# Five GpSimd transfers of weight rows, issued as single packets

## The chip, the cores and the metric

The kernel runs on one core of a Trainium2 chip. The metric is the device time of one execution in microseconds (us); less is better. The core has five engines with queues of their own: TensorE (PE) for matrix products, VectorE (DVE) and ScalarE (ACT) for elementwise work and reductions, GpSimd (POOL), and SyncE (SP), which here issues loads. Sixteen DMA engines move data between HBM and the on-chip memory. SyncE's transfers are queue q1 in the profile, GpSimd's are q0; both use the same sixteen engines.

## The reference

One decode step for 8 sequences with two branches on the same normalised input. Branch A is grouped-query attention over a cache of 4096 positions (32 query heads, 8 key/value heads of width 128); branch B is a gated MLP with 896 hidden units. All numbers are float32.

```python
xn = layernorm(x)                                   # x: 8 x 512
q  = xn @ wq                                        # 32 heads x 128
s  = softmax(q @ k_cache.T * 128**-0.5) @ v_cache   # per head; k, v: 8 x 8 x 4096 x 128
s  = s @ wo                                         # 8 x 512
z  = gelu(xn @ w_in)                                # 8 x 1792
z1, z2 = z[:896], layernorm(z[896:])
g  = silu((z1 * (w_sp * z2 + b_sp)) @ w_out)        # w_out: 896 x 512
out = x + s * g
```

The two caches are 268 MB of the 290 MB read.

## The kernel before

**Ring.** Large loads go through a ring of three slots of 64 KB per partition, 8.4 MB each over 128 partitions. SyncE issues the loads in program order: wq (slot 1), the MLP's weights (slot 2), kT(0,0) (slot 3), kT(0,1) (slot 1 again, once the query projection has read wq), v(0,0) (slot 2 again, once the MLP has read its weights), v(0,1), and so on for 8 heads, two halves each. `load_k` is lines 326 to 329, `load_v` lines 331 to 336. A load is issued when the last reader of the slot's earlier content is done.

**Order on TensorE.** `project_q(0)`, `project_q(1)` (lines 247 to 261), `mlp()` (167 to 245), then for each head `scores` (267 to 273), `softmax` and `values` (305 to 319). At the end the output projection with wo, whose last pieces are loaded in nine transfers of falling size.

**The MLP's slot** holds w_in, four of the seven 128-row blocks of w_out and a small side block. They come in one SyncE transfer, `w_mlp` (line 82). The other three blocks of w_out are taken out of it: the host packs their rows, as `w_ex`, into a region of the same slot (line 83), on partitions chosen row by row (the tables `LANES`, `ONES` and `RUNS`). Most of these rows come by four SyncE transfers (line 86). The rest come by five GpSimd transfers: `w_mid` (8 partitions of 14 KB, 112 KB) and `w_one0` to `w_one3` (3 partitions each, six pieces of 7 KB or 5 KB, so 42 or 30 KB). [...]

**Readers.** In `mlp()` the product with w_out is two loops: line 227 reads the four blocks of `w_mlp`, line 231 reads the seven units of `w_ex`. Line 231 is the last reader of the slot. Line 239 copies the side block on VectorE.

Of the kernel before, what the change touches and what calls it, by code (L numbers as in the profile page):

```python
# [14 lines left out]
B, D = 8, 512  # L15
# [9 lines left out]
QUAD = 4  # L25
# [20 lines left out]
def tile_gqa_gmlp_decode(ctx: ExitStack, tc: tile.TileContext, x, kT, v, wq, wo, w_mlp, w_ex0, w_ex1, w_ex2, w_ex3, w_mid, w_one0, w_one1, w_one2, w_one3, out, gate, stored):  # L46
    nc = tc.nc
# [27 lines left out]
    def from_slot(rows, n):  # L75
        lo = spare[0]
        spare[0] = lo + n
        return mlp_slot[:rows, lo:lo + n]
# [4 lines left out]
    w_ex = from_slot(P, UNITS * D).rearrange("p (u d) -> p u d", u=UNITS)  # L83
# [3 lines left out]
    turn = const.tile([4 * QUAD, 4, QUAD], F32, name="turn")  # L87
    queued = []

    def queue(dst, src):  # L90
        with tc.issue_after(queued[-1]) if queued else nullcontext():
            queued.append(nc.gpsimd.dma_start(dst, src).ins)

    def skip(i, k):
        queue(turn[:2 * k, i], w_mlp[:k, :4 * QUAD].rearrange("p (a q) -> p a q", a=2)[:, :, :QUAD])

    def one(i, src):
        p, u, n = ONES[i]
        queue(w_ex[p:p + 3, u:u + n].rearrange("p u d -> p (u d)").rearrange("p (c n) -> p c n", c=2),
              src[:, :3, :n * D // 2])  # L100

    skip(0, 7)
    queue(w_ex[60:68], w_mid[:, :QUAD])
    skip(1, 6)
    one(0, w_one0)
    skip(2, 7)
    one(1, w_one1)
    one(2, w_one2)
    skip(3, 6)
    one(3, w_one3)  # L110
# [242 lines left out]
    for h in range(HKV):  # L353
# [4 lines left out]
        for half in range(2):  # L358
# [11 lines left out]
            n = 2 if last else HALF  # L370
# [94 lines left out]
```

## Time and profile before

| | before |
|---|---|
| median of 3 runs | 689.87 us (689.77 to 689.96) |
| the profiled execution | 689.62 us, span 688.0 |
| granted TensorE clock, mean | 0.745 |
| PE busy | 341.1 us (50%) |
| read from HBM | 290.80 MB, 423 GB/s over the span |
| q1 (SyncE) | 6576 packets, 290.54 MB, 97.8% of 16 engines' span |
| q0 (GpSimd) | 656 packets, 0.27 MB, 0.1% |

The span runs from the first to the last instruction of the profiled execution; 1.6 us of its time lie around it. Times in the views count from the span's start. In the row of 40 slices each digit is the busy share of a slice of 17.2 us in tenths. In a group of instructions, the part behind the bar is busy time, mean ns of one, and the idle time just before, with what ended it. Line numbers are those of the kernel before.

### The profile page before, as it was taken

Reading aid. Unit: us, or ns where it says so; the run is one execution under the profiler, and the core shown is the slowest. Engines: PE = TensorE matmul, PEld = TensorE weight load, DVE = VectorE, ACT = ScalarE, POOL = GpSimd, SP = SyncE. Lnnn points to the kernel's source line nnn. Section 1 sums busy time; section 2 is a strip of 40 time slices with the busy share of each in tenths; the row PEclk is TensorE's granted clock in tenths of the full one; section 3 lists DMA queues with packets and bytes.
Section 4 is the critical chain, followed back from the end, with each engine's and each line's share of the span. In section 5 each row is a group of like instructions: output and inputs, shape, how many; then the busy total and the mean of one; then the engine's idle time right before and its main releaser. Section 6 shows DMA issues by size and latency. Waiting matters only on the chain.

```text
span 688.0 us, 5236 instructions
## 1 busy us (share of the span) xinstructions
PE 341.1 (50%) x2412; PEld 91.8 (13%) x2412; DVE 83.7 (12%) x163; ACT 13.4 (2%) x27; POOL 14.5 (2%) x26
## 2 busy tenths in 40 slices
PE   0353564555544445555544355555444445555558
PEld 0111121111111111111111011111101111111112
DVE  0133121100111021100201021100111021100221
ACT  0010000000000000000000000000000000000000
POOL 6100000000000000000000000000000000000000
PEclk9995597766776676777777667767776676777778
DMA  9999599999999999999999999999999999999997
GB/s 403 414 437 426 231 428 473 434 424 427 424 438 431 428 434 451 434 424 427 439 442 424 431 446 439 427 428 427 443 427 427 447 442 439 428 427 428 427 416 289
DMA packets 7397, 291.17 MB, mean 423 GB/s; under 512 B 1512, under 2 KB 1512, under 8 KB 2336
## 3 DMA queue, kind: packets, MB, share of 16 engines
q1 hardware_dynamic: 6576, 290.54, 97.8%
q8 instruction: 19, 0.31, 0.2%
q0 software_dynamic: 656, 0.27, 0.1%
q10 hardware_dynamic: 144, 0.03, 0.0%
q14 instruction: 2, 0.02, 0.0%
HBM read 290.80 MB, written 0.03 MB: 423 GB/s over the span
## 4 chain that ended last, share of the span: by engine, by line
DMA 73%; PE 18%; issue 4%; another core or an unknown queue 3%; DVE 1%; POOL 0%; SPq 0%; POOLq 0%
DMA slot<-in_kT 35%; DMA slot<-in_v 28%; PE sc L272 11%; DMA slot<-in_wo 7%; PE o_ps L313 6%; DMA slot<-in_x 3%; PE scr L227 1%; PE scr L231 1%; DVE slot L218 0%; PE scr L222 0%; POOL pick L134 0%; POOL slot L216 0%; SPq L335 0%; DVE rest L233 0%
## 5 line engine op out<-in xcount | busy, mean ns | idle before, releaser
L272 PE MATMUL sc<-slot,qz 128*32 128x512 f32 x1024 | 147.1, 739 | 127.0 <-DMA slot<-in_kT 127.0
L313 PE MATMUL o_ps<-slot,pT 128*16 128x512 f32 x1024 | 144.5, 728 | 110.5 <-DMA slot<-in_v 108.1
L272 PEld LDWEIGHTS sc<-slot,qz 128*32 128x32 f32 x1024 | 38.3, 132 | 229.3 <-issue 153.2
L313 PEld LDWEIGHTS o_ps<-slot,pT 128*16 128x16 f32 x1024 | 32.1, 112 | 208.8 <-issue 142.1
L277 DVE TENSOR_REDUCE nm<-sc 128x1 f32<-128x1024 f32 x8 | 9.8, 1225 | 271.2 <-PE sc L272 271.2
L316 DVE TENSOR_TENSOR o_all<-o_ps,diag 128x512 f32<-128x512 f32 x17 | 11.8, 692 | 241.7 <-PE o_ps L313 241.7
L279 ACT ACTIVATE p<-sc,nm 128x1024 f32<-128x1024 f32 x8 | 8.9, 1114 | 543.9 <-DVE nm L277 543.9
L323 PE MATMUL po_ps<-fold,o_sb 128*128 128x16 f32 x30 | 5.9, 273 | 26.8 <-DVE o_sb L318 26.8
L318 DVE TENSOR_REDUCE o_sb<-o_all 128x128 f32<-128x512 f32 x17 | 17.8, 1047 | 0.6
L162 PE MATMUL scr<-ident,slot 8*128 8x8 f32 x4 | 0.6, 255 | 28.0 <-DVE slot L159 28.0
L299 DVE STREAM_TRANSPOSE pT<-p 128x1024 f32<-128x1024 f32 x8 | 10.0, 1245 | 0.3
L323 PEld LDWEIGHTS po_ps<-fold,o_sb 128*128 128x128 f32 x30 | 4.5, 188 | 40.6 <-DVE o_sb L318 40.6
L252 PE MATMUL scr<-slot,xnT 128*32 128x512 f32 x64 | 9.7, 760 | 0.3 <-POOL slot L216 0.3
L231 PE MATMUL scr<-slot 128*32 128x512 f32 x14 | 3.6, 1058 | 11.8 <-DMA slot<-in_w_one 11.8
L347 PE MATMUL sc<-slot,oT 128*8 128x512 f32 (+1 forms) x60 | 8.2, 564 | 0.2 <-DMA slot<-in_wo 0.2
L282 PE MATMUL scr<-ident,nm 128*1 128x128 f32 x8 | 2.2, 270 | 10.8 <-DVE nm L277 10.8
L295 PE MATMUL scr<-wl,same 128*128 128x1 f32 x16 | 3.6, 297 | 6.5 <-DVE wl L293 6.5
L297 DVE TENSOR_SCALAR p<-p,w,wl 128x1024 f32<-128x1024 f32 x8 | 6.5, 813 | 0.3
L195 PE MATMUL scr<-part_sum,same 128*128 128x1 f32 x4 | 1.1, 348 | 8.4 <-DVE part_sum L193 8.4
L288 PE MATMUL scr<-ident,full 1*128 1x1 f32 x8 | 1.7, 219 | 5.1 <-DVE full L286 5.1
L162 PEld LDWEIGHTS scr<-ident,slot 8*128 8x128 f32 x4 | 0.5, 209 | 28.0 <-DVE slot L159 28.0
L295 PEld LDWEIGHTS scr<-wl,same 128*128 128x128 f32 x16 | 3.2, 249 | 7.0 <-PE scr L288 7.0
(97 smaller groups left out, 76.3 us busy)
## 6 DMA issues: line engine op xcount, KB each, us to landing
slot<-in_v SPq DMA_DIRECT2D x2, 4096.0 KB, 29.4
slot<-in_w_mlp SPq DMA_DIRECT2D x1, 4672.0 KB, 34.4
slot<-in_wo SPq DMA_DIRECT2D x1, 2048.0 KB
slot<-in_wo SPq DMA_DIRECT2D x1, 1536.0 KB
slot<-in_wo SPq DMA_DIRECT2D x1, 1280.0 KB, 39.7
slot<-in_wo SPq DMA_DIRECT2D x1, 1024.0 KB
slot<-in_wo SPq DMA_DIRECT2D x4, 256.0 KB, 19.1
slot<-in_wo SPq DMA_DIRECT2D x1, 768.0 KB
```

Source lines behind the costliest of these rows:

```text
L227: nc.tensor.matmul(pw[R * g:R * (g + 1), :], hT[:, R * g:R * (g + 1)], w_out_sb[:, g, :], start=True, stop=False)
L231: nc.tensor.matmul(pw[R * g:R * (g + 1), :], hE[:, i * R:(i + 1) * R], w_ex[:, i, :], start=False, stop=(i >= UNITS - G))
L252: nc.tensor.matmul(pq[R * g:R * (g + 1), :], xnT[:, k, :], wq_sb[:, k, lo:lo + REP * DH], start=(k == 0), stop=(k == NK - 1))
L272: nc.tensor.matmul(sc[R * g:R * (g + 1), c, :], qz[:, h, b * R:(b + 1) * R], k_sb[:, i, c, g, :], start=(b == 0), stop=(b == B - 1))
L277: nc.vector.tensor_reduce(m, sc, op=ALU.max, axis=AX.XY, negate=True)
L279: nc.scalar.activation(p, sc.rearrange("p c s -> p (c s)"), AF.Exp, bias=m, accum_out=l[:, h:h + 1])
L299: nc.vector.transpose(pT.rearrange("p j b g r -> p j g b r"), p.rearrange("p (j g b r) -> p j g b r", j=J, g=G, b=B))
L313: nc.tensor.matmul(of[R * c:R * c + G * REP, :], pT[:, j, b0 + i], v_sb[:, i, j], start=(j < rows), stop=(j >= J - rows))
L316: nc.vector.tensor_mul(o_all, o, diag[:, :, None].to_broadcast([P, G, DH]))
L318: nc.vector.tensor_reduce(o_sb, o_all.rearrange("p g d -> p d g"), op=ALU.add, axis=AX.X)
L323: nc.tensor.matmul(po[:, b0 * REP:(b0 + n) * REP], o_sb, f.rearrange("p i r -> p (i r)"), start=True, stop=True)
L347: nc.tensor.matmul(part[R * q:R * q + B, i * n:(i + 1) * n], oT[:, h, r, :], wo_sb[:, m, i * n:(i + 1) * n], start=(m < REP), stop=(cuts = ...
```

## The change

`queue` gets a third argument, `whole`, which it hands to the transfer as `single_packet`. It is set in the five transfers of w_out rows, `w_mid` and the four `w_one`, and not in the four `skip` transfers. [...] Sources, destinations, sizes and order stay, and on every engine the instructions stand in the same order as before.

```diff
-    def queue(dst, src):
+    def queue(dst, src, whole=False):
         with tc.issue_after(queued[-1]) if queued else nullcontext():
-            queued.append(nc.gpsimd.dma_start(dst, src).ins)
+            queued.append(nc.gpsimd.dma_start(dst, src, single_packet=whole).ins)
...
         queue(w_ex[p:p + 3, u:u + n].rearrange("p u d -> p (u d)").rearrange("p (c n) -> p c n", c=2),
-              src[:, :3, :n * D // 2])
+              src[:, :3, :n * D // 2], True)

     skip(0, 7)
-    queue(w_ex[60:68], w_mid[:, :QUAD])
+    queue(w_ex[60:68], w_mid[:, :QUAD], True)
     skip(1, 6)
     one(0, w_one0)
```

## The prediction

> **What bounds the kernel now.** I read the page first: its engine shares, the DMA row and the queues.
>
> ```profile
> PE 341.1 (50%) x2412; PEld 91.8 (13%) x2412; DVE 83.7 (12%) x163; ACT 13.4 (2%) x27; POOL 14.5 (2%) x26
> DMA  9999599999999999999999999999999999999997
> q1 hardware_dynamic: 6576, 290.54, 97.8%
> q0 software_dynamic: 656, 0.27, 0.1%
> ```
>
> TensorE works half the span; the sixteen DMA engines are busy in nearly every slice. The SyncE queue (q1) alone holds them for 97.8% of it. So this is a stream of 290 MB from HBM, and time can only be had where the stream stops. The DMA row has one such place: slice 5 (68.8 to 86.0 us) has a 5. GpSimd's queue (q0), which the change touches, carries 0.27 MB.
>
> Next, the stretches around that slice (columns: PE, PEld, DVE, ACT, POOL busy, clock, DMA share, GB/s):
>
> ```profile
> 60.00:70.00 10.00, 4.18 (x14) 0.90 (x12) 0.39 (x1) 0.00 (x0) 0.00 (x0) 0.50 0.97 417
> 70.00:82.00 12.00, 5.17 (x38) 1.55 (x42) 1.11 (x3) 0.26 (x1) 0.00 (x0) 0.50 0.47 178
> 82.00:90.00 8.00, 8.00 (x65) 2.25 (x60) 0.78 (x2) 0.00 (x0) 0.00 (x0) 0.81 0.91 393
> 90.00:640.00 550.00, 275.08 (x1918) 72.43 (x1908) 57.95 (x98) 11.26 (x24) 0.00 (x0) 0.73 1.00 433
> ```
>
> The undisturbed stream has share 1.00 and 433 GB/s. By share, 60 to 90 us lost 30 - (9.7 + 5.64 + 7.28) = 7.4 us. By bytes it moved 9.45 MB where 30 us at 433 GB/s would move 12.99; the missing 3.54 MB are 8.2 us. So the hole costs 7.4 to 8.2 us; I take 7.8.
>
> Why it is there is in the chain of waits (start, length, what), the group of line 231, and SyncE's own timeline:
>
> ```profile
> 62.32 1.86 PE scr L227 x6
> 64.18 11.74 another core or an unknown queue
> 76.01 3.69 PE scr L231 x14
> L231 PE MATMUL scr<-slot 128*32 128x512 f32 x14 | 3.6, 1058 | 11.8 <-DMA slot<-in_w_one 11.8
> 8.53 32.87 SPq L328 DMA_DIRECT2D slot<-in_kT  x2
> 79.76 10.63 SPq L335 DMA_DIRECT2D slot<-in_v  x2
> ```
>
> TensorE finishes the first half of the MLP's output product (L227) at 64.18 and then stands 11.8 us until the last w_one rows land. Line 231 is the last reader of the MLP's ring slot, so SyncE issues the next load, v(0,0), at 79.76, when line 231 has ended at 79.70. The load before it was issued by 41.4 us and ran out meanwhile.
>
> Why do 0.27 MB land so late? GpSimd's timeline and the landings of its transfers (KB each, us from issue to landing), in order of issue; the row with three numbers is for the two 30 KB ones:
>
> ```profile
> 1.35 0.76 POOL L92 DMA_DIRECT2D turn<-in_w_mlp  x1 [0.91 <-POOLq L453]
> 5.51 0.56 POOL L92 DMA_DIRECT2D slot<-in_w_mid  x1 [0.16 <-POOL ident masks.py:197]
> 6.07 0.56 POOL L92 DMA_DIRECT2D turn<-in_w_mlp  x1
> 6.63 0.63 POOL L92 DMA_DIRECT2D slot<-in_w_one  x1
> 7.26 0.57 POOL L92 DMA_DIRECT2D turn<-in_w_mlp  x1
> 7.83 1.24 POOL L92 DMA_DIRECT2D slot<-in_w_one  x2
> 10.75 0.62 POOL L92 DMA_DIRECT2D slot<-in_w_one  x1 [1.10 <-DMA turn<-in_w_mlp]
> ```
>
> ```profile
> turn<-in_w_mlp POOLq DMA_DIRECT2D x1, 0.2 KB, 9.1
> slot<-in_w_mid POOLq DMA_DIRECT2D x1, 112.0 KB, 19.1
> turn<-in_w_mlp POOLq DMA_DIRECT2D x1, 0.2 KB, 19.9
> slot<-in_w_one POOLq DMA_DIRECT2D x1, 42.0 KB, 29.1
> turn<-in_w_mlp POOLq DMA_DIRECT2D x1, 0.2 KB, 30.9
> slot<-in_w_one POOLq DMA_DIRECT2D x1, 30.0 KB, 47.3
> DMA to landing us min/median/max: 47.3/54.8/62.3
> slot<-in_w_one POOLq DMA_DIRECT2D x1, 42.0 KB, 65.2
> slot<-in_w_mlp SPq DMA_DIRECT2D x1, 4672.0 KB, 34.4
> ```
>
> Issue plus landing gives a ladder: first turn 10.5, w_mid 24.6, second turn 26.0, first w_one 35.7, third turn 38.2, second w_one 55.1, third 70.8 (issued at about 8.45), last 76.0. Now count packets. 656 packets over 16 engines are 41 each. The program's rows give the same number if every transfer puts the same count on every engine, with fillers where an engine has no data: a turn 1 + 1 for the semaphore, w_mid 4 + 1, each w_one 6 + 1; 4 x 2 + 5 + 4 x 7 = 41. A step of the ladder then costs: first w_one 9.7 us for 7 packets, 1.39 each; second w_one 16.9 us for 7, 2.42 each; third 15.7 for 7, 2.24 each. And one row of the main stream takes, at 433/16 = 27.1 GB/s an engine, 2.42 us if it is a 64 KB row of wq, kT or v, and 1.38 us if it is one of w_mlp's 36.5 KB rows (4672 KB over 128). The two prices are the two steps. So each small packet of q0 waits for one whole row of q1: **the engine alternates between the queues packet by packet, and it is the number of packets, not the bytes, that makes w_one late.**
>
> **The change part by part.** No instruction is added, removed or moved on any engine; five transfers get another packing.
>
> *Packets.* If a single packet is what it says, w_mid goes from 5 to 2 packets an engine, each w_one from 7 to 2: 18 instead of 41. The ladder, from the first turn at 10.5: eight more transfers of two packets each at 2.42 us are 38.7 us, plus the data itself on one engine. Its bounds: nothing, or all 256 KB on one engine, 9.7 us. That ends at 49 to 59 us, less where w_mlp's short rows stand between. Either end is before 64.18, when line 231 is ready, by 5 us or more. So the 11.8 us wait goes, all of it.
>
> *Bytes of w_one that now arrive earlier* push w_mlp's rows back on the engines that carry them. That is on the path:
>
> ```profile
> 25.13 0.68 DVE L155 BATCH_NORM_STATS2 st<-slot 8x6 f32<-8x512 f32 x1 [23.11 <-DMA slot<-in_x]
> 35.93 0.20 DVE L239 COPY x_out<-slot 128x64 f32<-128x64 f32 x1 [7.11 <-DMA slot<-in_w_mlp]
> 36.04 0.68 DVE L255 TENSOR_SCALAR q_sb<-scr 128x512 f32<-128x512 f32 x1
> ```
>
> VectorE's copy of line 239 waits for w_mlp (issued 1.55, 34.4 to landing), and behind it in VectorE's order stands line 255, which TensorE needs for everything up to line 227. What lands later here shifts 64.18 one for one. Bounds: nothing, if other engines are w_mlp's last; 5.4 us, if all 144 KB of the four w_one sat on the engine that is its last. I take one 30 KB transfer, 1.1 us: in before one 42 KB w_one had landed by 35.7 already, and the smallest further transfer on a loaded engine is 30 KB. x lands at 25.1, before most of it; I cost its shift at nothing, with the slack below as cover.
>
> *What is late next.* Without the wait, line 231 ends 11.8 us earlier, less 1.1: v(0,0) is issued at 79.76 - 10.7 = 69.1. When must it be there?
>
> ```profile
> 68.00:70.00 2.00, 0.00 (x0) 0.00 (x0) 0.00 (x0) 0.00 (x0) 0.00 (x0) 0.50 0.98 426
> 70.00:72.00 2.00, 0.00 (x0) 0.00 (x0) 0.00 (x0) 0.00 (x0) 0.00 (x0) 0.50 0.70 295
> 76.00:80.00 4.00, 3.64 (x14) 0.66 (x14) 0.28 (x1) 0.00 (x0) 0.00 (x0) 0.50 0.00 0
> 80.00:81.20 1.20, 0.73 (x20) 0.65 (x24) 0.42 (x1) 0.00 (x0) 0.00 (x0) 0.50 1.94 655
> ```
>
> A share of 1.94 is only possible if a packet counts where it starts. So the engines missing from 70 to 72 had their last packet start just before 70 and ran dry at about 72.2. The first bytes of v(0,0) come by 81.2, 1.4 us after its issue. Issued at 69.1 they come at 70.5, 1.7 us before the first engine is dry. The hole closes entirely. The next issue, v(0,1), needs the first half of the scores; it came 10.3 us after v(0,0) before, so about 80 now, with an 8 MB load (19.4 us at 433 GB/s) in front of it. No new hole.
>
> *What a larger packet costs.* It holds q1 off its engine for its bytes: 56 KB, half of w_mid, are 2.1 us. The bytes are the same as before, so the stream as a whole loses nothing.
>
> *Sum.* Nothing but the hole changes: -7.8 us (bounds -7.4 and -8.2). The profiled execution took 689.62 (span 688.0 and 1.6 around it); it would take 681.8, with a span of 680.2. The median of the runs is 689.87, 0.25 above, so 682.1.
>
> **The rivals.**
>
> *A, part of the hole stays.* w_mlp slips by the upper bound, 5.4 us: v(0,0) is issued at 73.3, its bytes come at 74.7, 2.5 us after the first engines ran dry. The gain is 7.8 - 2.5 = 5.3: 684.6. For it: w_mlp's landing sits on the path. Against: only one or two transfers can be in time to hurt it. 10%.
>
> *B, the flag does not change the order of service.* The packets are merged in name, but the engine still alternates row by row, or the packing falls back. Line 231 still waits 11.8 us: 689.9. Against: w_mlp's price and kT's price in the ladder show alternation by unit of packing, and 41 per engine fits that unit. 6%. [...]
>
> *C, slower: rows inside a big packet do not overlap.* Each row then pays its own trip. The nearest row for such a trip is the output store:
>
> ```profile
> out<-gate ACTq DMA_DIRECT2D x1, 32.0 KB, 1.5
> ```
>
> If the two 42 KB transfers share an engine, its 12 rows take 12 x 1.5 = 18 us where their 84 KB stream in 3.2: 14.8 us more on one engine, and every load of the stream waits for its slowest engine. Less the 7.8 of the hole: 7.0 slower, 696.9. It decides above 7.8/12 = 0.65 us more a row. For it: nothing measured. Against: rows follow each other at full rate in the stream (433 GB/s), with no such trip between them. 8%. [...]
>
> **How the numbers follow.** My forecast has 76%, A 10%, B 6%, C 8%. The time is that of the forecast, 682.1. Its own bounds are 681.7 to 682.5; drift of the engines against each other once they no longer restart together at 81 us can take or give about one microsecond, so 680.8 below. Upward the range takes in A with a little over: 684.8. B and C, 14%, stay outside. A change of 0.2% is 1.4 us, about what a measurement of this kernel can tell from none. Faster: forecast and A, 0.86. Same: B, 0.06. Slower: C, 0.08.
>
> **What would show it.** In the profile after, q0 has about 288 packets (18 x 16) for the same 0.27 MB; the last w_one lands before 60 us; line 231 no longer waits for w_one and starts at about 65; v(0,0) is issued near 69; the DMA row has no 5; the span is near 680. I am wrong if the packets fall and w_one still lands after 64, if w_mlp lands after 41 us (A), or if the hole is gone and some load later lands late (C).

## The result

The change does nothing. Over 12 executions each, the kernel after takes 689.69 us (689.36 to 690.32) and the one before 689.75 (689.33 to 690.28); the ratio of after to before is 0.9999, 95% interval 0.999 to 1.0008. The profiled execution has a span of 688.3 us against 688.0. The prediction, 682.1 in a range of 680.8 to 684.8, missed.

The page of the kernel after, the lines that answer to those shown of before:

```profile
DMA  9999599999999999999999999999999999999997
q1 hardware_dynamic: 6576, 290.54, 97.8%
q0 software_dynamic: 656, 0.27, 0.1%
L231 PE MATMUL scr<-slot 128*32 128x512 f32 x14 | 3.6, 1058 | 11.9 <-DMA slot<-in_w_one 11.9
```

The third line decides. q0 still has 656 packets, 41 an engine, where the prediction had 288. Slice 5 is still a 5, and line 231 still waits 11.9 us for w_one. The stretches, the last w_one's issue and landing, and SyncE's next load show the same hole at the same place:

```profile
70.00:82.00 12.00, 5.05 (x42) 1.39 (x46) 1.20 (x4) 0.26 (x1) 0.00 (x0) 0.59 0.47 178
90.00:640.00 550.00, 271.53 (x1900) 71.74 (x1888) 58.80 (x99) 11.25 (x24) 0.00 (x0) 0.74 1.00 433
10.83 0.61 POOL L92 DMA_DIRECT2D slot<-in_w_one  x1 [1.19 <-DMA turn<-in_w_mlp]
slot<-in_w_one POOLq DMA_DIRECT2D x1, 42.0 KB, 65.2
79.87 8.39 SPq L335 DMA_DIRECT2D slot<-in_v  x2
```

The last w_one lands at 76.0 as before, v(0,0) is issued at 79.87 (79.76 before), and the DMA engines stand idle for half of 70 to 82 us.

Why the packets did not change can be read one level down. Nine of GpSimd's transfers stand at line 92: w_mid, the four w_one and four turns, transfers of 0.2 KB that `skip` issues into the tile `turn`, whose data nobody reads. In the kernel's own description of them the flag is set on five of nine; in the compiled program it is gone. GpSimd's instructions, and those of the other four engines, are byte for byte the same before and after. The chip ran one program twice.

### The profile page after: what moved, and what is told of

The parts are those of the page before. It is cut to its first block, busy times and chain, and to the rows that moved or that the text cites. A ratio compares the mean times of both kernels' runs of the same rounds, so it can differ in the third digit from the quotient of the medians.

```text
span 688.3 us, 5236 instructions
## 1 busy us (share of the span) xinstructions
PE 335.6 (49%) x2412; PEld 91.0 (13%) x2412; DVE 83.7 (12%) x163; ACT 13.4 (2%) x27; POOL 14.5 (2%) x26
## 3 DMA queue, kind: packets, MB, share of 16 engines
q1 hardware_dynamic: 6576, 290.54, 97.8%
## 4 chain that ended last, share of the span: by engine, by line
DMA 78%; PE 14%; issue 4%; another core or an unknown queue 2%; DVE 1%; POOL 0%; SPq 0%; POOLq 0%
DMA slot<-in_kT 36%; DMA slot<-in_v 32%; DMA slot<-in_wo 7%; PE o_ps L313 6%; PE sc L272 6%; DMA slot<-in_x 3%; PE scr L227 1%; PE scr L231 1%; DVE slot L218 0%; PE scr L222 0%; POOL pick L134 0%; POOL slot L216 0%; SPq L335 0%; DVE st L155 0%
## 5 line engine op out<-in xcount | busy, mean ns | idle before, releaser
L272 PE MATMUL sc<-slot,qz 128*32 128x512 f32 x1024 | 140.1, 710 | 128.6 <-DMA slot<-in_kT 128.6
L313 PE MATMUL o_ps<-slot,pT 128*16 128x512 f32 x1024 | 147.0, 738 | 113.1 <-DMA slot<-in_v 113.1
L231 PE MATMUL scr<-slot 128*32 128x512 f32 x14 | 3.6, 1058 | 11.9 <-DMA slot<-in_w_one 11.9
```

The source lines that it names most:

```text
L231: nc.tensor.matmul(pw[R * g:R * (g + 1), :], hE[:, i * R:(i + 1) * R], w_ex[:, i, :], start=False, stop=(i >= UNITS - G))
L272: nc.tensor.matmul(sc[R * g:R * (g + 1), c, :], qz[:, h, b * R:(b + 1) * R], k_sb[:, i, c, g, :], start=(b == 0), stop=(b == B - 1))
L313: nc.tensor.matmul(of[R * c:R * c + G * REP, :], pT[:, j, b0 + i], v_sb[:, i, j], start=(j < rows), stop=(j >= J - rows))
```

## The experiments

Two questions were left. Is the flag really lost, or does it only fall back for long rows? And was the rest of the argument right, that the count of packets, times one row of the main stream, holds w_one back, and that the hole is worth 7.8 us? If so, another way to pass the packets must bring the time that the flag did not.

Each kernel below is compared with the kernel before, run beside it on the same chip: 689.68 us beside `double`, `left_out`, `spread` and `no_turns`, 689.49 beside `k_halves`, `k_quarters` and `shifted`, 689.58 in the one execution beside `double_flag`. A ratio is the kernel's time over that of the kernel before.

### Short pieces, with and without the flag

`double` cuts w_one1 and w_one2 into 12 pieces of 2.5 KB each; `double_flag` is the same with the flag on the five transfers.

```diff
-        queue(w_ex[p:p + 3, u:u + n].rearrange("p u d -> p (u d)").rearrange("p (c n) -> p c n", c=2),
-              src[:, :3, :n * D // 2])
+        c = 4 if i in (1, 2) else 2
+        queue(w_ex[p:p + 3, u:u + n].rearrange("p u d -> p (u d)").rearrange("p (c n) -> p c n", c=c),
+              src[:, :3 * c // 2, :n * D // c])
...
```

The host packs the rows to match (left out here).

> w_one1 and w_one2 are cut into 12 pieces each instead of 6; bytes, engines and order stay. Packets theory: 53 packets an engine, 848 in all. If the alternation held to the end, 12 packets more at 2.4 us would land the last w_one at about 105 us; but when the main stream runs dry at 74 to 77 us nothing is left to alternate with and the rest follows at once: the last lands at 77 to 80 us, line 231 starts there, and the time is 690.5 to 693 us. So the hole limits itself: more packets cost little, fewer gain much. GpSimd theory: no change beyond 1 us, 689 to 691.

> The kernel with w_one1 and w_one2 in 12 pieces of 2.5 KB, with the flag on the same five transfers as in the change. Without the flag GpSimd frames two such pieces a packet (656 packets in all, 12 of them of 5120 B). If the flag works and only fell back because the rows of 5 and 7 KB are too long for a common packet, the short pieces give it room: fewer than 656 packets and data packets of more than 5120 B for w_one1 and w_one2, landing before 76. If the flag does not reach the chip at all: 656 packets again, the same landings within half a microsecond, the same time within 1 us.

`double` took 689.66 us (ratio 0.9999, 0.999 to 1.0009), below the 690.5 to 693 that were expected. Its packet row, and under it that of `double_flag`:

```profile
q0 software_dynamic: 656, 0.27, 0.1%
```

```profile
q0 software_dynamic: 656, 0.27, 0.1%
```

The expectation of 848 packets for `double` was wrong: twelve short pieces make six packets, the same as six pieces twice as long. Pieces are packed together without being asked: with 656 packets in both runs, two of 2.5 KB went into a packet where one of 5 KB went before. So this run did not try what it was meant to try, the cost of more packets. `double_flag` has 656 again, its landings are within 0.2 us of those of `double`, and its one execution took 689.48 beside 689.58. With room for more pieces in a packet the flag still changes nothing: it does not fall back for length, it has no effect.

### The hole without w_one

`left_out` leaves out the four w_one transfers, so those rows of w_out stay zero. w_mid and the four turns stay.

```diff
     queue(w_ex[60:68], w_mid[:, :QUAD])
     skip(1, 6)
-    one(0, w_one0)
     skip(2, 7)
-    one(1, w_one1)
-    one(2, w_one2)
     skip(3, 6)
-    one(3, w_one3)
```

> The four w_one transfers are left out (144 KB, so those rows of w_out stay zero); w_mid and the four turns stay. It gives the price of the hole with no w_one at all. Packets theory: 13 packets an engine, 208 in all; line 231 starts near 64 us, the hole closes, 681 to 683 us, about the same as with w_one on fewer packets (the fullest engines keep their load). Given-back theory: 688 or more. If this one closes the hole and the kernel with 3 whole rows does not, the packet count is not the cause.

680.05 us, ratio 0.986 (0.9846 to 0.9875). The stretches, SyncE's next load and q0's packets:

```profile
60.00:70.00 10.00, 9.13 (x81) 3.38 (x84) 2.28 (x6) 0.26 (x1) 0.00 (x0) 0.81 0.99 427
70.00:82.00 12.00, 8.47 (x68) 2.37 (x64) 0.00 (x0) 0.00 (x0) 0.00 (x0) 0.86 1.00 433
82.00:90.00 8.00, 4.42 (x36) 1.50 (x28) 2.71 (x7) 1.41 (x3) 0.00 (x0) 0.86 0.95 410
65.07 8.40 SPq L331 DMA_DIRECT2D slot<-in_v  x2
q0 software_dynamic: 208, 0.12, 0.1%
```

Without w_one nothing stops the stream, and 9.6 us go, a little more than expected. The time is not given back later.

### The same packets beside shorter rows

If each of q0's packets waits for one row of the main stream, shorter rows must let them pass. `k_halves` loads kT(0,0) and kT(0,1) in two transfers each, of 32 KB rows; `k_quarters` in four, of 16 KB (there `parts` is 4). GpSimd's nine transfers are untouched, in the same order, with no flag.

```diff
-        nc.sync.dma_start(t, kT[h, half])
+        parts = 2 if h == 0 else 1
+        n = SLOT // parts
+        for c in range(parts):
+            nc.sync.dma_start(t[:, c * n:(c + 1) * n], kT[h, half][:, c * n:(c + 1) * n])
```

> kT(0,0) and kT(0,1) are loaded as two transfers each, of 32 KB rows; GpSimd's nine transfers are those of the kernel before, on the same engines, without the flag. Packets theory: q0 keeps 656 packets, but from about 38 us on each waits for a 32 KB row, 1.21 us, instead of 2.42; some 16 packets are left then, so the last w_one lands at about 58 to 63 us, just before line 231 is ready; the hole closes almost or fully, and with no engine loaded otherwise the time is 681 to 683.5 us. If what counts is bytes or GpSimd, nothing changes: landing 76, 689.7. Given-back theory: wait gone, time above 688.

> The same with four transfers of 16 KB rows for each of the two loads. Packets theory: each of the last 16 packets waits 0.6 us plus its own data; the last w_one lands at about 49 to 54 us; line 231 does not wait; 681 to 683 us, the same as with halves or a little better, since the wait is gone in either. If shorter rows cost the stream speed, it shows here: every further 1% on these 16.8 MB is 0.4 us.

`k_halves`: 680.30 us (680.19 to 680.38), ratio 0.9865 (0.9848 to 0.9881). `k_quarters`: 680.60, ratio 0.9869 (0.9854 to 0.9884). Both are a little below the 681 that was expected at best. The page of `k_halves`, the issue and landing of its last w_one, line 231, and the next load:

```profile
DMA  9999999999999999999999999999999999999997
q1 hardware_dynamic: 6864, 290.54, 99.1%
q0 software_dynamic: 656, 0.27, 0.1%
10.86 0.61 POOL L92 DMA_DIRECT2D slot<-in_w_one  x1 [1.21 <-DMA turn<-in_w_mlp]
slot<-in_w_one POOLq DMA_DIRECT2D x1, 42.0 KB, 52.7
L231 PE MATMUL scr<-slot 128*32 128x512 f32 x14 | 3.5, 1038 | 0.0
67.92 7.53 SPq L338 DMA_DIRECT2D slot<-in_v  x2
```

The same 656 packets now are through at 10.86 + 52.7 = 63.6 us instead of 76.0, and line 231, which starts at 64.2, has no wait. Up to 36 us, while the neighbours are the same rows as before, the two queues start equally many packets; the kernel before, 10 to 36 us:

```profile
q1 hardware_dynamic: 303, 10.90, 97.0%
q0 software_dynamic: 303, 0.16, 2.1%
```

From 36 to 48 us, beside the rows of kT, q0 starts 113 packets in the kernel before, 190 in halves and 290 in quarters:

```profile
q0 software_dynamic: 113, 0.02, 0.9%
```

```profile
q0 software_dynamic: 190, 0.04, 1.7%
```

```profile
q0 software_dynamic: 290, 0.08, 2.9%
```

GpSimd's transfers are the same in all three, and only the rows beside them are shorter, and so more. So it is the alternation, row by row, that made w_one late. v(0,0) is issued at 67.92 (the prediction had said 69.1), the 5 in the DMA row is gone, and q1 keeps the engines busy for 99.1% of the span instead of 97.8%. In quarters the last w_one is earlier still (39.5 us from issue, so at 50.2) and buys nothing, 680.60 us against 680.30 in halves, where it was there before line 231 was ready too. One thing beside the rows moved: with the loads cut, some matmuls of the first scores stand ahead of line 227. `left_out`, where TensorE's order has the scores behind the MLP as before, gained about as much.

### Fewer packets by other means

`spread` writes each w_one as 3 whole rows and has only three turns. `no_turns` leaves out the four turns; the five transfers of w_out rows stay. Both compute everything.

```diff
-        queue(w_ex[p:p + 3, u:u + n].rearrange("p u d -> p (u d)").rearrange("p (c n) -> p c n", c=2),
-              src[:, :3, :n * D // 2])
+        queue(w_ex[p:p + 3, u:u + n].rearrange("p u d -> p (u d)"), src[:, :n * D])
...
     one(0, w_one0)
-    skip(2, 7)
+    one(3, w_one3)
+    skip(2, 2)
     one(1, w_one1)
     one(2, w_one2)
-    skip(3, 6)
-    one(3, w_one3)
...
```

> Each w_one is written as 3 whole rows instead of 6 half rows, so it falls on three engines with one row each; the order is changed so that three turns are enough. All the work is done. Packets theory (an engine alternates between the queues row by row, so the count of q0's packets sets when the last w_one lands): 19 packets an engine, 304 in all; the last w_one lands between 40 and 51 us; line 231 starts at about 64 without a wait for w_one; the hole at 70 to 82 us closes and the time is 682 to 683 us, of which about half a microsecond goes to the engines that now carry 14 KB more. GpSimd theory (w_one is late because GpSimd makes or starts the transfers late, or because its bytes are slow): the last lands near 76 as before and the time is 689.8. Given-back theory (the wait goes but the time does not): the last w_one lands before 55, line 231 does not wait, and the time is still above 688 because a later load is late by as much.

> [...] The result is computed in full. Packets theory: 33 packets an engine, 528 in all; the last w_one lands 10 to 16 us earlier, at 60 to 66 us; most of the hole closes, and the time is 684 to 687 us, since engines 0 to 2 now carry up to 56 KB more (2.1 us). GpSimd theory: less than 1 us of change in the landing (four issues of 0.6 us less on GpSimd), time 689 to 690 or worse by the 2.1 us of the fuller engines. Given-back theory: landing as in the packets theory, time 689 or more.

`spread`: 685.28 us, ratio 0.9937 (0.9922 to 0.9951). `no_turns`: 692.29, ratio 1.0037 (1.0024 to 1.005). The packets and VectorE's wait for w_mlp, of `spread`:

```profile
q0 software_dynamic: 304, 0.26, 0.1%
39.31 0.20 DVE L237 COPY x_out<-slot 128x64 f32<-128x64 f32 x1 [9.69 <-DMA slot<-in_w_mlp]
72.76 8.40 SPq L333 DMA_DIRECT2D slot<-in_v  x2
```

and of `no_turns`, with its wait in front of the loop that was line 231:

```profile
q0 software_dynamic: 528, 0.26, 0.1%
38.58 0.20 DVE L235 COPY x_out<-slot 128x64 f32<-128x64 f32 x1 [7.99 <-DMA slot<-in_w_mlp]
PE scr L227 <- DMA slot<-in_w_one: 8.7, 1, 8.7
```

The packet counts are exactly those foretold, 19 x 16 and 33 x 16. In `spread` they leave 2 an engine for a w_one instead of 7, as one row on each of three engines would. There w_one no longer holds line 231 and the hole closes, but only 4.4 us come of it, where 682 to 683 had been expected. The MLP is later (w_mlp is there at 39.31 instead of 35.93), but from 70 to 82 us the DMA share is 0.99, so the later MLP by itself stops nothing. The stream itself has lost the time, at both ends. The first 90 us of `spread` and, under them, of `k_halves`, then the last 13 us of `spread`:

```profile
0.00:90.00 90.00, 40.83 (x286) 13.65 (x286) 18.18 (x54) 2.17 (x3) 13.48 (x25) 0.87 1.00 414
```

```profile
0.00:90.00 90.00, 41.29 (x290) 14.29 (x290) 21.55 (x61) 3.58 (x6) 14.48 (x26) 0.86 1.00 425
```

```profile
670.70:683.70 13.00, 9.22 (x134) 2.55 (x126) 3.18 (x7) 0.00 (x0) 0.00 (x0) 0.97 0.54 215
```

With the engines as busy (share 1.00 in both), 11 GB/s less over 90 us are 1.0 MB, or 2.3 us of the stream. At the end the engines are busy for 0.54 of the time, against 0.73 in `k_halves` (its row stands further down), which is 2.5 us. Together they are 4.8 of the 5.0 us between the two spans. In `no_turns` the gain was expected and did not come. The last w_one lands later than before, near 78 us, not at 60 to 66. The third lands at 60.1, 10.7 us earlier than before, as fewer packets would have it; the last then takes 18.0 us more, where before it took 5.2. That was a fault of the expectation: before, the last w_one's six pieces met a stream that had run dry (DMA share 0.55 from 72 to 74 us, 0.04 from 74 to 76) and no longer had to alternate, so the ladder's end at 76 was too early as a base to subtract from. To this comes again a slow start, w_mlp at 38.58; how much each part weighs was not measured. The profile names the engine of no packet, so the expectation's 56 KB more on engines 0 to 2, worth 2.1 us, was the author's estimate and no run shows it.

### A shorter first turn

The author has the turns choose the engines of the transfers behind them; no run shows that they do. Both kernels with fewer turns gave up some of that choice. `shifted` keeps all 41 packets an engine and gives the first turn 10 rows instead of 14, so that by this account the five transfers of w_out rows fall on other engines.

```diff
-    skip(0, 7)
+    skip(0, 5)
```

> [...] It asks what slowed the kernels with fewer turns early on (w_mlp landed 3 us later than before in both). Engine theory (a transfer that falls on an engine other than the one the turns choose slows the others' rows): w_mlp lands 2 us or more later than 35.9 and the time is 690.5 to 693. Load theory (it was only the additional bytes on engines that were full already): w_mlp lands within 1 us of 35.9 and the time is 689 to 690.5.

691.92 us, ratio 1.004 (1.0027 to 1.0053). The waits for x and for w_mlp, of `shifted`:

```profile
q0 software_dynamic: 656, 0.27, 0.1%
27.17 0.68 DVE L155 BATCH_NORM_STATS2 st<-slot 8x6 f32<-8x512 f32 x1 [25.15 <-DMA slot<-in_x]
38.07 0.20 DVE L239 COPY x_out<-slot 128x64 f32<-128x64 f32 x1 [7.20 <-DMA slot<-in_w_mlp]
```

With the packets the same, x lands 2.0 us later and w_mlp 2.1, and the kernel loses 2.4. So the first turn's length has a price of its own, and the load theory's ranges are missed; the engine theory's are met. Why it is so stays open. Rows may be slow on another engine than the one the turns choose, or the engines that take the transfers may have less to spare: half of w_mid, 56 KB, is 2.1 us of one engine at 27.1 GB/s (an estimate from the 433 GB/s over sixteen), as much as x and w_mlp slip. The runs show the loss and not its seat.

## Why the prediction was wrong, step by step

- **Where the time could come from: right.** The one hole, its cause (line 231's wait for w_one holds the ring slot, and with it v(0,0)) and its reason (q0 alternates with q1 packet by packet, 303 and 303 from 10 to 36 us) all stand: `k_halves` changed only the rows beside it and closed the hole, and `left_out` closed it without w_one.
- **"w_mid goes from 5 to 2 packets an engine, each w_one from 7 to 2: 18 instead of 41": this step failed.** It rested on "if a single packet is what it says", the flag taken at its name; no run shows the 2 packets or the 18. In their place the packets stayed 656, 41 an engine, before and after, and with short pieces too, so the wait of line 231 stayed 11.9 us. The condition was written down, given 6% against in rival B, and everything behind it was built on it. B was the case, by its second reading and more simply than it said: nothing fell back, since the flag is not in the program that runs.
- **The weight of the evidence.** The ladder proved that packets set the landing. It could say nothing of whether the flag sets packets; no row of before has a transfer with the flag on. A term on which the whole sum hangs, and which no row shows, deserved more than 6% against.
- **The price of the hole: 7.8, measured 9.2** where the same wait was taken away with all loads kept (`k_halves`, span 688.0 to 678.7). The 7.8 was the idle time in the hole. Most of the rest is at the end. The last 13 us, before (first row) and in `k_halves` (second):

```profile
675.00:688.00 13.00, 10.07 (x142) 2.99 (x134) 3.18 (x7) 0.00 (x0) 0.00 (x0) 0.98 0.61 246
```

```profile
665.70:678.70 13.00, 9.30 (x138) 2.74 (x130) 3.17 (x7) 0.00 (x0) 0.00 (x0) 0.99 0.73 294
```

  The share rises from 0.61 to 0.73, which over 13 us is 1.6 us. So the engines are busier at the end where the hole was taken away with GpSimd's transfers untouched; `left_out` has 0.71 there. Why, no run shows, and it is no rule: `spread` has no hole either and ends with 0.54. The prediction had put such drift at "about one microsecond" either way.
- **w_mlp's shift, 1.1 us: not put to the test.** In `k_halves` the small transfers come early only after w_mlp has landed. In `spread` they come with it and w_mlp slips by 3.4 us, but there they are cut otherwise too (2 packets an engine for a w_one instead of 7).
- **"What is late next": right.** In `k_halves` v(0,0) was issued at 67.92, and the stretches behind it, from 70 to 640 us, run at share 1.00 or more, so no later load stopped the stream.
- **Rivals A and C** never came into play. Their condition, large packets, did not occur. What a packet of several rows, 30 to 56 KB, costs stays open; no run here has one.

## What to carry to other kernels

Where a flag is the whole change, first find out that it reaches the instructions: compare the compiled programs, or count in the profile what it should change (here one number, q0's packets). In this kernel a small transfer beside a saturated stream paid by the packet, one row of the other queue for each (2.42 us beside rows of 64 KB); if one is late, shorten the rows that run beside it rather than its own bytes. Cutting two 8 MB loads in half took 9.2 of 689.5 us, where a flag meant for the small transfers took nothing.

## What the runs showed of the hardware

- Beside a full stream the two queues took turns packet by packet: 303 and 303 from 10 to 36 us, in the kernel before. A packet of GpSimd's waited 1.39 us beside 36.5 KB rows and 2.42 beside 64 KB rows (the steps of the ladder).
- GpSimd's packets in all fit the same number on each of the 16 engines: 41 x 16, 33 x 16, 19 x 16 and 13 x 16 were counted to the packet, three of them foretold. Taken from each other these counts give 2 an engine for a turn, 5 for w_mid, 7 for a w_one of six pieces, and, with 2 for each of its three turns, 2 for a w_one of three rows in `spread`. What the packets beyond those of data are for, no run shows, and the profile names the engine of none.
- Short pieces shared a packet: 12 pieces of 2.5 KB gave as many packets as 6 of 5 KB, 656 in all. Why two, no run tests.
- 32 KB and 16 KB rows in two of the loads cost next to nothing: 680.3 and 680.6 us, with 288 and 864 packets more on q1, beside 680.05 in `left_out`, whose rows stay at 64 KB.
- A first turn of 10 rows instead of 14, with the same 656 packets, cost 2.4 us.
